# Attention with a KV cache on one core: 16 KB loads, a block transpose on VectorE, P*V in 32-row array tiles, and the projection in token groups

## The chip, the cores and the metric

The kernel runs on one core of one Trainium2 chip. The time is the device time of one execution in microseconds. A kernel's time is the median of its runs; a comparison is a ratio with a 95% interval, from runs of both kernels on the same chip.

## The reference

32 sequences, 4 new tokens each (128 tokens in all), 32 query heads on 4 key/value heads, 2048 cached keys of width 128, all in bfloat16:

```python
B, Sq, D = 32, 4, 1024
Hq, Hkv, Sk, Dh = 32, 4, 2048, 128
q = (x @ wq).reshape(B, Sq, Hq, Dh).transpose(0, 2, 1, 3)
k, v = repeat(k_cache, 8, axis=1), repeat(v_cache, 8, axis=1)
scores = einsum("bhqd,bhkd->bhqk", q, k) * Dh ** -0.5
o = einsum("bhqk,bhkd->bhqd", softmax(scores), v)
out = o.transpose(0, 2, 1, 3).reshape(B, Sq, Hq * Dh) @ wo
```

K and V are 67.1 MB each, `wq` and `wo` 8.4 MB each: 151 MB to read for very little arithmetic. "Batch" below means one of the 32 sequences. Its 4 tokens x 32 heads are 128 rows of scores, 32 for each key/value head.

## The kernel before

For each batch: K is transposed on TensorE in eight "fills" of eight 128x128 transposes into a ring of four PSUM banks; VectorE and ScalarE evacuate the fills to `KT_sb`; the score product fills `ps_s`; VectorE takes the maximum and ScalarE the exponential; P is transposed on TensorE by a product with a diagonal that also normalises; P*V uses the whole array, 128 keys per weight load. One projection of all 128 tokens ends the kernel.

```python
# loads: rows of 16 keys x 128 x 2 bytes = 4 KB
def k_src(b): return k_cache[b].rearrange("g (p t) d -> p g (t d)", p=128)
def v_src(b): return v_cache[b].rearrange("g (p t) d -> p g (t d)", p=128)
# SyncE: four K loads a batch, one for each key/value head, two batches ahead
# GpSimd: one V load a batch, after P*V of batch b - 3, and one 256 KB piece of wo
...
def do_tr_fills(b):                     # P transposed and normalised on TensorE
    wait exp(b), diag(b)
    for f in range(4):
        ring_wait(j)
        for q in range(4):
            t = f * 4 + q
            eng.matmul(dst[:, q * 128:(q + 1) * 128],
                       lhsT=P_sb[:, t * 128:(t + 1) * 128], rhs=diag[:, b % 2, :])
...
def do_pv(b):                           # 4 x 16 = 64 pairs of weight load and matmul
    for g in range(G):
        for t in range(NKT):
            eng.matmul(ps_o[:, 32 * g:32 * (g + 1)],
                       lhsT=V_sb[:, vs, g, t * Dh:(t + 1) * Dh],
                       rhs=PT_sb[:, t, 32 * g:32 * (g + 1)],
                       start=(t == 0), stop=(t == NKT - 1))
...
for i in range(B):                      # order of TensorE's program
    qk(i)                               # 4 column tiles of 32, 16 matmuls of 512 columns
    if i >= 1: do_pv(i - 1)
    if i + 2 < B: do_kt_fills(i + 2)
    do_tr_fills(i)
do_pv(B - 1)
for c in range(2):                      # the projection, once, at the end
    for h in range(Hq):
        eng.matmul(ps_s[:, c * 512:(c + 1) * 512], lhsT=oT_sb[:, h, :],
                   rhs=wo_view[:, h, c * 512:(c + 1) * 512], ...)
```

(Waits and marks are cut, and the calls are shortened.)

## Time and profile before

| kernel before | |
|---|---|
| time, median of 2 runs | 410.25 us (409.25 to 411.25) |
| profiled span, granted clock | 409.6 us, 0.925 |
| bytes read | 151.3 MB, 402 to 408 GB/s from slice 5 to slice 36 |
| tail with hardly any load | about 37 us, of it 16.0 us projection |

These lines are from the profile's page. In it PE is TensorE's matmuls, PEld its weight loads, DVE VectorE, ACT ScalarE, POOL GpSimd, SP SyncE. The first four give the span, the busy time of each engine, and two rows of the table of 40 equal slices of 10.2 us (granted TensorE clock in tenths; GB/s of all loads). Then comes the queue that carries the engines' own instructions (packets, MB, share), and the engines' shares of the chain that ended last.

```profile
span 409.6 us, 12650 instructions
PE 306.7 (75%) x5448; PEld 251.4 (61%) x5448; DVE 244.7 (60%) x390; ACT 197.2 (48%) x230; POOL 42.0 (10%) x70
...
PEclk9799799998999899999999999997998989889679
...
GB/s 307 400 387 401 408 408 407 407 406 407 407 407 408 405 406 407 406 407 407 408 404 407 407 407 406 407 407 406 407 406 407 407 407 408 403 402 308 38 2 26
...
q8 instruction: 44, 0.72, 0.7%
...
DMA 53%; PE 28%; issue 6%; SPq 5%; DVE 4%; ACT 3%; ACTq 0%; DVEq 0%
```

The flat row of GB/s, 402 to 408 from slice 5 to slice 36, says that the loads bind: no compute engine is above 75%. The end of the row is the tail. Queue 8: 44 packets of 16 KB, each 256 instructions of TensorE (5448 matmuls and as many weight loads are 42.6 such blocks).

Next are groups of instructions: count, then busy us and mean ns of one, then the engine's idle time just before them and what ended most of it.

```profile
L539 ACT ACTIVATE pp_sb<-ps_s,negmx 128x2048 bf16<-128x2048 f32 x32 | 62.9, 1967 | 98.7 <-DVE negmx L484 98.7
L481 DVE TENSOR_REDUCE mx<-ps_s 128x1 f32<-128x2048 f32 x32 | 73.3, 2292 | 43.8 <-PE ps_s L397 43.8
...
L346 PE MATMUL ps_o<-pp_sb,V_sb 128*128 128x32 bf16 x2048 | 57.4, 178 | 11.5 <-DMA V_sb<-in_v_cache_dram 7.0
...
L397 PE MATMUL ps_s<-KT_sb,QT_sb 128*32 128x512 bf16 x512 | 34.7, 391 | 2.6 <-ACT QT_sb L522 0.8
```

The view of waits sums, for each engine and line, what it waited for (us in all, times, longest):

```profile
PE ps_c L312 <- DMA K_sb<-in_k_cache_dram: 15.1, 13, 1.6
...
PE ps_b L312 <- issue: 7.9, 4, 2.6
PE ps_a L312 <- issue: 7.6, 3, 2.9
```

"Issue" is time in which an engine waits for nothing that the profile shows. Where do those stops come from? In the instruction records of TensorE, 16 gaps of over 0.3 us (27 us in all, median 1.75) lie at one and the same place, the 193rd of every 256 instructions. After 15 of the 16, TensorE goes on 2.3 to 2.6 us after a packet of queue 8 starts. So they belong to the fetch of instructions, not to the data.

The timeline of the end gives start, duration, engine, line and operation:

```profile
388.14 1.87 PE L346 MATMUL ps_o<-pp_sb,V_sb 128*128 128x32 bf16 x64 [0.88 <-ACT pp_sb L446]
...
390.44 15.95 PE L418 MATMUL ps_s<-w_sb,oT_sb 128*128 128x512 bf16 x64 [0.43 <-issue]
```

### The profile page before, as it was taken

To read this page: it belongs to the slowest core of one execution; us is meant where nothing else is said; L and a number is where in the kernel's file an instruction comes from. 1 tells how busy PE (TensorE), PEld (TensorE's weight loads), DVE (VectorE), ACT (ScalarE), POOL (GpSimd) and SP (SyncE) were. 2 spreads that over 40 slices of the span, in tenths; PEclk is the share of its full clock that TensorE was granted. 3 is DMA by queue.
4 is the path that set the end of the run, shared out by engine and by line. 5 is a ranking of instruction groups with operands and counts; after the bars stand their busy time and mean duration, and the time that the engine had idled before them with its cause. 6 is when DMAs were issued, how large, how long until landed. Compare 5 with 4: busy or idle time off the path is not lost.

```text
span 409.6 us, 12650 instructions
## 1 busy us (share of the span) xinstructions
PE 306.7 (75%) x5448; PEld 251.4 (61%) x5448; DVE 244.7 (60%) x390; ACT 197.2 (48%) x230; POOL 42.0 (10%) x70
## 2 busy tenths in 40 slices
PE   4576877988777687577777777759876787775596
PEld 4476766867655576466666566548765676674442
DVE  2113286786666587677766776745875867765400
ACT  1213066474555555555555455553555555545300
POOL 0001011110100111111111111110110111120000
PEclk9799799998999899999999999997998989889679
DMA  8999999999999999999999999999999999997000
GB/s 307 400 387 401 408 408 407 407 406 407 407 407 408 405 406 407 406 407 407 408 404 407 407 407 406 407 407 406 407 406 407 407 407 408 403 402 308 38 2 26
DMA packets 42390, 152.33 MB, mean 372 GB/s; under 512 B 3168, under 2 KB 3168, under 8 KB 42336
## 3 DMA queue, kind: packets, MB, share of 16 engines
q0 software_dynamic: 19456, 75.50, 46.3%
q1 hardware_dynamic: 21728, 71.84, 44.7%
q10 hardware_dynamic: 1152, 4.19, 2.6%
q8 instruction: 44, 0.72, 0.7%
q14 instruction: 10, 0.08, 0.1%
HBM read 151.26 MB, written 0.26 MB: 370 GB/s over the span
## 4 chain that ended last, share of the span: by engine, by line
DMA 53%; PE 28%; issue 6%; SPq 5%; DVE 4%; ACT 3%; ACTq 0%; DVEq 0%
DMA K_sb<-in_k_cache_dram 32%; DMA V_sb<-in_v_cache_dram 15%; DMA w_sb<-in_wq_dram 6%; PE ps_o L346 5%; PE ps_s L418 4%; PE ps_o L312 4%; PE ps_s L397 3%; SPq L278 3%; PE ps_c L312 3%; PE ps_a L312 3%; PE ps_b L312 2%; SPq L283 2%; ACT KT_sb L446 2%; DVE mx L481 2%; PE ps_s L371 2%
## 5 line engine op out<-in xcount | busy, mean ns | idle before, releaser
L539 ACT ACTIVATE pp_sb<-ps_s,negmx 128x2048 bf16<-128x2048 f32 x32 | 62.9, 1967 | 98.7 <-DVE negmx L484 98.7
L481 DVE TENSOR_REDUCE mx<-ps_s 128x1 f32<-128x2048 f32 x32 | 73.3, 2292 | 43.8 <-PE ps_s L397 43.8
L346 PEld LDWEIGHTS ps_o<-pp_sb,V_sb 128*128 128x128 bf16 x2048 | 53.9, 96 | 25.9 <-issue 16.6
L346 PE MATMUL ps_o<-pp_sb,V_sb 128*128 128x32 bf16 x2048 | 57.4, 178 | 11.5 <-DMA V_sb<-in_v_cache_dram 7.0
L312 PE MATMUL ps_c<-ident,K_sb 128*128 128x128 bf16 x512 | 43.6, 232 | 19.7 <-DMA K_sb<-in_k_cache_dram 15.1
L268 POOL DMA_DIRECT2D V_sb<-in_v_cache_dram x32 | 23.8, 745 | 303.1 <-PE ps_o L346 274.4
L312 PE MATMUL ps_a<-ident,K_sb 128*128 128x128 bf16 x512 | 43.3, 232 | 13.7 <-issue 7.6
L444 DVE COPY KT_sb<-ps_b 128x1024 bf16<-128x1024 bf16 x64 | 43.7, 684 | 12.0 <-PE ps_b L312 11.9
L446 ACT ACTIVATE KT_sb<-ps_a 128x1024 bf16<-128x1024 bf16 x32 | 32.6, 1019 | 37.1 <-PE ps_a L312 37.0
L312 PE MATMUL ps_b<-ident,K_sb 128*128 128x128 bf16 x512 | 43.9, 233 | 7.9 <-issue 7.9
L312 PEld LDWEIGHTS ps_c<-ident,K_sb 128*128 128x128 bf16 x512 | 34.1, 105 | 21.6 <-DMA K_sb<-in_k_cache_dram 19.5
L312 PE MATMUL ps_o<-ident,K_sb 128*128 128x128 bf16 x512 | 43.1, 232 | 3.2 <-DVE KT_sb L444 3.1
L312 PEld LDWEIGHTS ps_a<-ident,K_sb 128*128 128x128 bf16 x512 | 32.9, 104 | 17.6 <-issue 12.0
L446 ACT ACTIVATE KT_sb<-ps_c 128x1024 bf16<-128x1024 bf16 x32 | 32.7, 1022 | 20.9 <-PE ps_c L312 20.9
L312 PEld LDWEIGHTS ps_b<-ident,K_sb 128*128 128x128 bf16 x512 | 34.7, 105 | 9.1 <-issue 8.5
L312 PEld LDWEIGHTS ps_o<-ident,K_sb 128*128 128x128 bf16 x512 | 34.2, 105 | 6.9 <-DVE KT_sb L444 4.4
L444 DVE CAST pp_sb<-ps_a 128x512 bf16<-128x512 f32 x32 | 22.1, 691 | 27.2 <-PE ps_a L328 27.2
L397 PE MATMUL ps_s<-KT_sb,QT_sb 128*32 128x512 bf16 x512 | 34.7, 391 | 2.6 <-ACT QT_sb L522 0.8
L446 ACT ACTIVATE KT_sb<-ps_o 128x1024 bf16<-128x1024 bf16 x32 | 32.7, 1023 | 0.0
L444 DVE COPY KT_sb<-ps_a 128x1024 bf16<-128x1024 bf16 x32 | 21.9, 685 | 10.2 <-PE ps_a L312 10.2
L371 PE MATMUL ps_s<-pp_sb,w_sb 128*128 128x128 bf16 x256 | 19.8, 255 | 10.0 <-DMA w_sb<-in_wq_dram 10.0
L371 PEld LDWEIGHTS ps_s<-pp_sb,w_sb 128*128 128x128 bf16 x256 | 19.2, 118 | 10.6 <-DMA w_sb<-in_wq_dram 10.6
(36 smaller groups left out, 288.9 us busy)
## 6 DMA issues: line engine op xcount, KB each, us to landing
V_sb<-in_v_cache_dram POOLq DMA_DIRECT2D x32, 2048.0 KB, 26.4
K_sb<-in_k_cache_dram SPq DMA_DIRECT2D x120, 512.0 KB, 14.6
w_sb<-in_wq_dram SPq DMA_DIRECT2D x4, 2048.0 KB, 25.2
w_sb<-in_wo_dram POOLq DMA_DIRECT2D x32, 256.0 KB, 26.1
K_sb<-in_k_cache_dram ACTq DMA_DIRECT2D x8, 512.0 KB, 10.7
pp_sb<-in_x_dram SPq DMA_DIRECT2D x1, 256.0 KB, 4.2
out_dram<-pp_sb SPq DMA_DIRECT2D x1, 256.0 KB, 2.0
```

The costliest lines, as they stand in the source:

```text
L268: eng.dma_start(V_sb[:, vs, :, :], v_src(b)).then_inc(s_v[vs], 16)
L278: eng.dma_start(wq_sb[:, :, c * WQC:(c + 1) * WQC], wq_v[:, :, c * WQC:(c + 1) * WQC]).then_inc(s_wq[c], 16)
L283: eng.dma_start(K_sb[:, ks, g, :], k_src(b)[:, g, :]).then_inc(s_k[ks][g], 16)
L312: ins = eng.transpose(dst[:, q * 128:(q + 1) * 128], K_sb[:, ks, g, t * Dh:(t + 1) * Dh], ident[:, :],)
L346: ins = eng.matmul(ps_o[:, 32 * g:32 * (g + 1)], lhsT=V_sb[:, vs, g, t * Dh:(t + 1) * Dh], rhs=PT_sb[:, t, 32 * g:32 * (g + 1)], start=(t ...
L371: ins = eng.matmul(ps_s[:, col:col + 128], lhsT=wq_sb[:, kt, h * Dh:(h + 1) * Dh], rhs=xT_sb[:, kt, :], start=(kt == 0), stop=(kt == KT - 1),)
L397: ins = eng.matmul(ps_s[32 * g:32 * (g + 1), c * 512:(c + 1) * 512], lhsT=QT_sb[:, i, REP * g:REP * (g + 1), :], rhs=KT_sb[:, kts, g, c * ...
L418: ins = eng.matmul(ps_s[:, c * 512:(c + 1) * 512], lhsT=oT_sb[:, h, :], rhs=wo_view[:, h, c * 512:(c + 1) * 512], start=(h == 0), stop=(h ...
L444: ins = eng.tensor_copy(dst, src)
L446: ins = eng.activation(dst, src, ACT.Copy)
L481: ins = eng.tensor_reduce(mx[:, i:i + 1], ps_s[:, :], AX.X, ALU.max)
L539: ins = eng.activation(P_sb, ps_s[:, :], ACT.Exp, bias=negmx[:, i:i + 1], scale=scale, accum_out=ssum[:, i:i + 1],)
```

## The change

The whole kernel is written anew. The intent: larger rows for the loads, no transposing of P on TensorE, no long projection at the end.

- K and V are loaded with 64 neighbouring keys of one head in each partition: rows of 16 KB. Partition 32g + r holds keys 64r to 64r + 63 of head g.
- So the keys of a head lie on 32 partitions only. P is normalised and transposed in 32x32 blocks on VectorE, and P*V contracts 32 keys at a time on a 32-row tile of the array: 64 steps x 4 heads = 256 pairs instead of 64.
- P*V writes the first 32 columns of the four ring banks, so it waits for the last K evacuations, and the next fills wait for O's evacuation (now on ScalarE, ahead of the exponential).
- `wq` is loaded first and alone, in 16 KB rows; all loads are in one queue. `wo` is loaded early.
- The projection runs for 32 tokens at a time after batches 7, 15, 23 and 31, in four column tiles.

```diff
-            return v_cache[b].rearrange("g (p t) d -> p g (t d)", p=128)
+                V_sb[:, b % NVB, :, :], v_cache[b].rearrange("g (r t) d -> (g r) t d", r=R)),
 ...
-                        ins = eng.matmul(dst[:, q * 128:(q + 1) * 128],
-                            lhsT=P_sb[:, t * 128:(t + 1) * 128], rhs=diag[:, b % 2, :])
+            p.op("dve", lambda e: e.tensor_scalar(P_sb[:, :], P_sb[:, :], rinv[:, i:i + 1], None, op0=ALU.mult), ...)
+            p.op("dve", lambda e: e.transpose(PT_sb[:, i % 2, :, :].rearrange("p t q -> p (t q)"), P_sb[:, :]), ...)
 ...
-                    for t in range(NKT):                      # 16 for each of 4 heads
-                        ins = eng.matmul(ps_o[:, 32 * g:32 * (g + 1)],
-                            lhsT=V_sb[:, vs, g, t * Dh:(t + 1) * Dh],
-                            rhs=PT_sb[:, t, 32 * g:32 * (g + 1)], ...)
+            for t in range(T):                                # 64 for each of 4 heads
+                for g in range(G):
+                    p.op("pe", lambda e, t=t, g=g: e.matmul(ps_r[:, g, 0:32],
+                        lhsT=V_sb[32 * g:32 * (g + 1), i % NVB, t, :],
+                        rhs=PT_sb[32 * g:32 * (g + 1), i % 2, t, :], ...), ...)
 ...
+            for h in range(Hq):                               # oproj(n): tokens 32n to 32n + 31
+                for j in range(4):
+                    p.op("pe", lambda e, h=h, j=j: e.matmul(ps_r[32 * j:32 * (j + 1), 0, 0:NC],
+                        lhsT=oT_sb[:, h, 32 * n:32 * (n + 1)],
+                        rhs=wo_sb[:, h, NC * j:NC * (j + 1)], tile_position=(0, 32 * j), ...), ...)
 ...
+        for i in range(B):                                    # order of the programs
+            pe_qk(i); softmax_max(i)
+            if i >= 1: pe_pv(i - 1); ot(i - 1)
+            if i + AHEAD < B: pe_fills(i + AHEAD)
+            if i >= 1 and i % OG == 0: oproj(i // OG - 1)
+            softmax_exp(i); ev(i + AHEAD, dve_fs); ev(i + AHEAD, act_fs)
+            softmax_pt(i)
```

(Cut and shortened; the remainder is the same algorithm in another frame.)

## The prediction

> **What bounds the kernel now.** DMA. In the 40 slices it moves a flat 405 to 408 GB/s from the start to slice 36: 151.3 MB, 372 of 409.6 us. The rest is a tail after the last V lands (timeline: two softmax rounds, the last P*V, a projection of 16.0 us). No compute engine is at its limit (PE 75%, DVE 60%, ACT 48%); one batch costs 10.3 us of DMA.
>
> **What the change takes away.**
> - DMA: packet records show 86 ns for 2 KB, 162 ns for 4 KB, so about 10 ns fixed. For 16 KB I estimate 618 ns, 424 GB/s: 357 us in all.
> - Start: wq comes first and alone, so batch 0 starts about 12 us sooner. Tail: only the last token group's projection, 4 to 5 us instead of 16.
> - 16 P-transposing matmuls and four evacuations per batch.
>
> Were DMA still the bound: about 375 us. I don't think it will be.
>
> **What it adds, per batch.**
> - P*V becomes 256 weight-load/matmul pairs instead of 64. On the whole array pairs start 25.2 ns apart (P*V's records). [...]this trace's score matmuls agree (3.3 ns between column tiles). So P*V takes about 2 us if row tiles overlap, 6.5 us if not.
> - VectorE: normalising P [...]and the block transpose. [...]I estimate [...]like the max reduction: 2.3 us.
> - A serial loop. P*V writes the ring banks, so it waits for K's last evacuations; ScalarE does O's evacuation, exp, then five evacuations, in order. From the end of one P*V to the start of the next: 0.45 + 2.2 + 5 x 0.92 = 7.3 us on ScalarE; via evacuation 5, normalisation and transpose about 8.5 us on VectorE. Period = P*V + 8.5 us: 10.5 us at best.
> - Instructions: PE goes from about 350 to 690 per batch. PE's program comes in 16 KB blocks (256 instructions; queue 8, 44 packets). In the records PE stops at the same place of every 256 when a fetch is late, and resumes 2.4 to 2.6 us after its packet starts; under full DMA load fetches are never less than 6.4 us apart. Now that is hidden under DMA ("issue", 0.9 to 3 us a stop). After, a P*V of 512 instructions outruns the fetched blocks once or twice per batch, estimate 2 to 5 us each batch.
>
> So the period is 12.5 to 15.5 us (middle 14), above the 9.9 us of DMA: 32 x 14 + 33 us start + 10 us tail = about 490 us.
>
> **Predicted: 490 us, range 385 to 565. Faster by over 2%: 0.25; within 2%: 0.05; slower by over 2%: 0.70.**
>
> **What would show it.** DMA near 300 GB/s in the middle; 16 KB packets of about 620 ns (if still 4 KB, no gain of rate). Queue 8 near 90 packets. The chain of waits made of VectorE transpose, ScalarE evacuations, P*V and "issue" in P*V. P*V's matmuls in bursts 6 ns apart with stops of 2 to 5 us. Start and tail together some 20 us shorter: right even if the total is wrong.
>
> **What would make it wrong.** If fetches are quicker with fewer data queues or further ahead, and row tiles overlap fully, the period is about 10.5 us, the time 375 to 390 us. If row tiles don't overlap, or a 32-row weight load is slow, or the clock halves in the waits, it passes 540 us.

The forecast's sum came to 490 us: 32 periods of 14 us, 33 us of start, 10 us of tail. The 14 us are P*V's 2, the loop's 8.5 and, in the middle, 3.5 for late fetches. The trace before shows this: score matmuls in neighbouring column tiles start 4 ns apart in the median (294 of 384 steps 1 to 5 ns, the others 14 to 18; the 3.3 ns are near the first four of a batch, 3.1 in the mean). With two starts of 4 ns for each pair of weight load and matmul, 256 pairs would take 2.0 us (an estimate; that row tiles overlap in the same way was the assumption). The maximum over 2048 columns takes 2.29 us, from which the transpose is estimated. The 2.2 us are the exponential and the read of its sum (1.97 and 0.19 us); evacuations on ScalarE start some 0.92 us apart. The 0.45 us for O's evacuation are the estimate (VectorE took 0.28 us for it before).

## More of the kernel before

On one core a single run has no known state (fast or slow). The runs told here as "one look" are such single runs, each beside one run of the kernel before, and are used only where the difference is far larger than a few per cent.

## The result

| | before | after |
|---|---|---|
| median time | 410.25 us (2 runs) | 609.08 us (2 runs, 606.88 to 611.28) |
| ratio | 1 | 1.4848 (1.4695 to 1.5001) |
| profiled span, clock | 409.6 us, 0.925 | 605.1 us, 0.718 |
| stops at the 193rd of 256 instructions | 16, 27 us | 45, 176 us |

A ratio is the mean time of one kernel's fast runs over the mean of the other's of the same rounds, so it is not quite the ratio of the medians quoted beside it.

The page after, with the same lines as before and the queue that carries the loads added:

```profile
span 605.1 us, 23784 instructions
PE 329.0 (54%) x11528; PEld 291.8 (48%) x11528; DVE 246.4 (41%) x265; ACT 229.7 (38%) x261; POOL 7.1 (1%) x18
...
PEclk9997675777767677776667876757777766777756
...
GB/s 367 427 430 418 238 386 393 364 338 246 235 154 279 214 264 222 239 226 222 244 263 277 283 135 178 273 260 278 263 234 226 236 168 279 249 218 234 142 3 8
...
q1 hardware_dynamic: 14192, 151.29, 63.4%
q8 instruction: 90, 1.47, 0.9%
...
PE 41%; issue 29%; DVE 20%; DMA 6%; ACT 3%; SPq 0%
```

No engine and no queue is at its limit any more (PE 54%, the queue of the loads 63.4%). The loads reach 427 to 430 GB/s while the buffers fill in the first slices, more than before, and from the tenth slice on fall to between 135 and 283, because the buffers come free too late (SyncE waits 503 us in all for the fills before it can issue the next K). The chain of waits has lost the loads (53% to 6%) and gained "issue" (6% to 29%). The instruction queue carries 90 packets instead of 44 (11528 matmuls and as many weight loads are 90.1 blocks of 256).

The groups after:

```profile
L207 PE MATMUL ps_r<-ident,K_sb 128*128 128x128 bf16 x2048 | 184.4, 276 | 35.7 <-ACT oT_sb L254 14.3
L246 PE MATMUL ps_r<-PT_sb,V_sb 32*128 32x32 bf16 x8192 | 78.1, 182 | 221.1 <-issue 150.8
...
L273 DVE STREAM_TRANSPOSE PT_sb<-P_sb 128x2048 bf16<-128x2048 bf16 x32 | 74.0, 2311 | 1.1
...
L271 DVE TENSOR_SCALAR P_sb<-P_sb,rinv 128x2048 bf16<-128x2048 bf16 x32 | 24.1, 754 | 1.1
```

The waits after:

```profile
PE ps_r L246 <- issue: 150.8, 37, 5.5
PE ps_r L246 <- DVE PT_sb L273: 70.3, 32, 5.7
...
PE ps_r L207 <- issue: 14.0, 7, 3.9
```

P*V waits 150.8 us for "issue" in 37 stops, about one a batch: its own instructions are late. The timeline shows it. Two batches follow each other here, and below them the last batch:

```profile
303.54 1.23 PE L246 MATMUL ps_r<-PT_sb,V_sb 32*128 32x32 bf16 x133 [1.93 <-DVE PT_sb L273]
...
308.74 1.18 PE L246 MATMUL ps_r<-PT_sb,V_sb 32*128 32x32 bf16 x123 [3.97 <-issue]
...
309.99 0.28 ACT L254 ACTIVATE oT_sb<-ps_r 128x128 bf16<-128x128 f32 x1 [7.84 <-PE ps_r L246]
310.17 1.96 ACT L265 ACTIVATE P_sb<-ps_s,negmx 128x2048 bf16<-128x2048 f32 x1
...
310.42 0.69 PE L207 MATMUL ps_r<-ident,K_sb 128*128 128x128 bf16 x5 [0.49 <-ACT oT_sb L254]
...
314.83 6.05 PE L207 MATMUL ps_r<-ident,K_sb 128*128 128x128 bf16 x59 [3.73 <-issue]
...
321.22 2.31 DVE L273 STREAM_TRANSPOSE PT_sb<-P_sb 128x2048 bf16<-128x2048 bf16 x1
...
323.59 1.62 PE L246 MATMUL ps_r<-PT_sb,V_sb 32*128 32x32 bf16 x180 [1.73 <-DVE PT_sb L273]
...
330.03 0.79 PE L246 MATMUL ps_r<-PT_sb,V_sb 32*128 32x32 bf16 x76 [4.82 <-issue]
...
591.35 1.67 PE L246 MATMUL ps_r<-PT_sb,V_sb 32*128 32x32 bf16 x181 [5.69 <-DVE PT_sb L273]
...
595.40 0.79 PE L246 MATMUL ps_r<-PT_sb,V_sb 32*128 32x32 bf16 x75 [2.38 <-issue]
...
596.59 5.41 PE L284 MATMUL ps_r<-w_sb,oT_sb 128*32 128x256 bf16 x128 [0.40 <-ACT oT_sb L254]
```

P*V does 133 pairs in about 1.2 us, stands still for 4 us, and does the other 123. While it stands, ScalarE and the fills wait behind it (the 7.84 us before O's evacuation), so the stop is paid in full. The stop moves by 47 pairs from one batch to the next (133, then 180): from one P*V to the next TensorE has 674 instructions in the records (932 or 930 where a projection lies between). That is 94 short of three blocks of 256, so a stop that stays at the same place of each 256 moves by 94 instructions, or 47 pairs. In the last batch no loads run, and the stop is 2.4 us.

The start times in the records give one batch, as a mean over batches 0 to 27: period 18.0 us, of which P*V takes 7.3 us from its first to its last start (5.3 us of stops, 2.0 us of matmuls), and 10.7 us pass from there to the next P*V.

### The profile page after: what moved, and what is told of

It reads as the page before. It is cut to its first block, busy times and chain, and to the rows that moved or that the text cites. A ratio compares the mean times of both kernels' runs of the same rounds, so it can differ in the third digit from the quotient of the medians.

```text
span 605.1 us, 23784 instructions
## 1 busy us (share of the span) xinstructions
PE 329.0 (54%) x11528; PEld 291.8 (48%) x11528; DVE 246.4 (41%) x265; ACT 229.7 (38%) x261; POOL 7.1 (1%) x18
## 3 DMA queue, kind: packets, MB, share of 16 engines
q1 hardware_dynamic: 14192, 151.29, 63.4%
## 4 chain that ended last, share of the span: by engine, by line
PE 41%; issue 29%; DVE 20%; DMA 6%; ACT 3%; SPq 0%
PE ps_r L207 25%; PE ps_r L246 13%; DVE PT_sb L273 12%; DMA K_sb<-in_k_cache_dram 6%; DVE P_sb L271 4%; DVE KT_sb L219 3%; PE ps_r L284 3%; ACT oT_sb L254 2%; ACT P_sb L265 1%; ACT KT_sb L221 1%; DVE rinv L270 0%; SPq L127 0%; DVE o_sb L292 0%; SPq L124 0%
## 5 line engine op out<-in xcount | busy, mean ns | idle before, releaser
L207 PE MATMUL ps_r<-ident,K_sb 128*128 128x128 bf16 x2048 | 184.4, 276 | 35.7 <-ACT oT_sb L254 14.3
L246 PE MATMUL ps_r<-PT_sb,V_sb 32*128 32x32 bf16 x8192 | 78.1, 182 | 221.1 <-issue 150.8
L207 PEld LDWEIGHTS ps_r<-ident,K_sb 128*128 128x128 bf16 x2048 | 178.0, 129 | 40.5 <-issue 32.2
L246 PEld LDWEIGHTS ps_r<-PT_sb,V_sb 32*128 32x128 bf16 x8192 | 71.3, 94 | 240.4 <-issue 154.3
L219 DVE COPY KT_sb<-ps_r 128x1024 bf16<-128x1024 bf16 x96 | 66.4, 691 | 290.0 <-PE ps_r L207 290.0
L221 ACT ACTIVATE KT_sb<-ps_r 128x1024 bf16<-128x1024 bf16 x160 | 155.0, 1025 | 44.6 <-PE ps_r L207 42.1
L273 DVE STREAM_TRANSPOSE PT_sb<-P_sb 128x2048 bf16<-128x2048 bf16 x32 | 74.0, 2311 | 1.1
L265 ACT ACTIVATE P_sb<-ps_s,negmx 128x2048 bf16<-128x2048 f32 x32 | 62.8, 1961 | 1.5 <-DVE negmx L261 1.5
L271 DVE TENSOR_SCALAR P_sb<-P_sb,rinv 128x2048 bf16<-128x2048 bf16 x32 | 24.1, 754 | 1.1
L284 PE MATMUL ps_r<-w_sb,oT_sb 128*32 128x256 bf16 x512 | 16.6, 292 | 3.5 <-issue 2.6
```

The costliest lines, as they stand in the source:

```text
L207: p.op("pe", lambda e, b=b, f=f, q=q, t=t: e.transpose(ring[f % 4][:, q * 128:(q + 1) * 128], K_sb[:, b % NKB, t, :], ident[:, :]), waits ...
L219: p.op("dve", lambda e: e.tensor_copy(dst, src), waits, ("kt", b, f))
L221: p.op("act", lambda e: e.activation(dst, src, ACT.Copy), waits, ("kt", b, f))
L246: p.op("pe", lambda e, t=t, g=g: e.matmul(ps_r[:, g, 0:32], lhsT=V_sb[32 * g:32 * (g + 1), i % NVB, t, :], rhs=PT_sb[32 * g:32 * (g + 1), ...
L265: p.op("act", lambda e: e.activation(P_sb[:, :], ps_s[:, :], ACT.Exp, bias=negmx[:, i:i + 1], scale=scale, accum_out=ssum[:, i:i + 1]), [( ...
L271: p.op("dve", lambda e: e.tensor_scalar(P_sb[:, :], P_sb[:, :], rinv[:, i:i + 1], None, op0=ALU.mult), [("rinv", i)], ("pn", i))
```

## The experiments

The theory (A): TensorE's instructions arrive too slowly. A batch has twice as many, a fetch of 256 comes too late, and each late fetch stops P*V for about 5 us. The rivals: (B) the chain of steps through VectorE and ScalarE makes the period by itself, with P*V's matmuls a small part; (A2) a stop is as long without loads as with them; (A3) it is long because the fetch stands behind 16 KB data packets. The first four runs are one look each, on one chip, beside one run of the kernel before of 408.97 us.

### A quarter of P*V (e1_quarter_pv)

Wrong (relative error 0.83): only 64 of the 256 pairs of each batch, all else as after.

```diff
-            for t in range(T):
+            for t in range(T // 4):
```

> The changed kernel with P*V cut to a quarter (64 of 256 pairs per batch; a wrong result on purpose; loads, transposes, softmax, evacuations unchanged). Theory A, instruction supply: PE now runs about 306 instructions per batch, P*V fits in what is already fetched, its stops of 5 us vanish; with the stops gone the clock stays higher and K's transposes shorten; the period falls under 10 us and the loads bind: 370 to 410 us. Theory B, the serial loop between P*V, ScalarE and VectorE: only P*V's own 2.0 us shrink to 0.5: 605 - 32 x 1.5 = about 555 us.

Measured: 406.02 us (span 404.2, clock 0.873). No stop in P*V is left, and queue 8 has 42 packets. Theory A's interval holds, B's does not. A transposing matmul of K takes 242 ns in the mean instead of 276. TensorE's largest waits are now for the transposed P and for evacuations; in six places the fills wait for K:

```profile
PE ps_r L246 <- DVE PT_sb L273: 71.6, 32, 7.1
...
PE ps_r L207 <- DMA K_sb<-in_k_cache_dram: 25.8, 6, 6.5
```

The timeline of one batch of this run:

```profile
304.24 2.25 DVE L260 TENSOR_REDUCE mx<-ps_s 128x1 f32<-128x2048 f32 x1
304.37 0.56 PEld L246 LDWEIGHTS ps_r<-PT_sb,V_sb 32*128 32x128 bf16 x64 [2.59 <-DVE PT_sb L273]
...
306.72 1.97 ACT L265 ACTIVATE P_sb<-ps_s,negmx 128x2048 bf16<-128x2048 f32 x1 [1.32 <-DVE negmx L261]
...
308.68 4.67 ACT L221 ACTIVATE KT_sb<-ps_r 128x1024 bf16<-128x1024 bf16 x5
...
310.40 0.69 DVE L219 COPY KT_sb<-ps_r 128x1024 bf16<-128x1024 bf16 x1 [2.52 <-PE ps_r L207]
...
311.99 2.31 DVE L273 STREAM_TRANSPOSE PT_sb<-P_sb 128x2048 bf16<-128x2048 bf16 x1
...
314.35 0.56 PEld L246 LDWEIGHTS ps_r<-PT_sb,V_sb 32*128 32x128 bf16 x64 [2.59 <-DVE PT_sb L273]
```

This is the serial loop without stops: maximum, exponential, ScalarE's first evacuation, the fill behind it, VectorE's last evacuation, normalisation, transpose, and the next maximum waits for that transpose. It takes 9.98 us, and P*V runs beside the maximum. The loads of a batch need about 9.9 us (an estimate: 4.19 MB at the 424 GB/s of the prediction). So A's guess that the loads would bind holds only in part: the loop sets the pace of most batches, the loads that of a few early ones (18.7 us of the waits for K fall while `wo` lands, up to 121 us), and the three projections add some 5 to 8 us each. Without stops this design came to 406 us: the faster loads are given back. (The quarter takes 0.5 us where the whole P*V takes 2.0. That the whole one would still fit beside the 2.25 us maximum is argued, not run.)

### Half of P*V twice (e2_more_pairs)

Correct: the first half of P*V is done, then the whole of it over again; 384 pairs a batch.

```diff
-            for t in range(T):
+            for n, t in enumerate(list(range(T // 2)) + list(range(T))):
```

> The changed kernel with the first half of P*V done twice (384 pairs per batch, result stays right). Theory A: 256 more instructions are one more fetched block per batch, about 5.2 us: 605 + 32 x 5.2 = about 770 us (740 to 800), and some 122 packets on queue 8. Theory B: 128 pairs more at 8 ns are 1.0 us per batch: about 640 us.

Measured: 739.4 us (clock 0.678), a hair under A's interval; B's is far off. Queue 8 has 122 packets; 73 stops at the 193rd instruction take 282 us. The same wait as above:

```profile
PE ps_r L246 <- issue: 262.8, 69, 6.1
```

The 256 more instructions of a batch cost (739.4 - 609.1) / 32 = 4.1 us, and the array needs 1.0 us for them (128 pairs at 8 ns). Three points lie close to one line: 290 instructions from one P*V to the next gave 406 us, 674 gave 609, 930 gave 739 (16.5 and 15.9 ns for each added instruction).

### No loads after the first buffers (e3_no_loads)

Wrong (relative error 1.10): K is loaded for batches 0 and 1 and V for 0 to 2 only; later batches use what lies in the buffers.

```diff
+            if b >= NKB:
+                p.at[("k", b)] = p.at[("k", b % NKB)]
+                return
 ... (the same for V)
```

> The changed kernel with K and V loaded for the first two and three batches only (wrong result on purpose; instructions of PE unchanged). If a late block waits behind the loads' packets (theory A1), the stop in P*V falls from 5.0 us to about 2.5 us, as in the last three batches of the changed kernel: 605 - 32 x 2.7 = about 515 us (490 to 530). If a block takes as long whatever the load (A2): 590 to 605 us.

Measured: 506.94 us (clock 0.757), in A's interval, outside A2's. There are as many fetches (90 packets), but 38 stops take 88 us, median 2.36 instead of 4.65. The period is 14.5 us.

```profile
PE ps_r L252 <- issue: 77.3, 35, 5.3
```

The loads thus cost half of the stop. From the start of a fetch's packet to TensorE going on, it is 2.4 us in this run as in the run after (median 2.44 and 2.36); the added time lies before the packet starts. Even with almost no loads this kernel is 98 us slower than the kernel before.

### Rows of 4 KB (e4_4kb_rows)

Correct: each K and V load in four parts, with rows of 4 KB instead of 16 KB.

```diff
-            p.dma("sp", lambda e: e.dma_start(K_sb[:, b % NKB, :, :], ...))
+            for c in range(4):
+                p.dma("sp", lambda e, c=c: e.dma_start(K_sb[:, b % NKB, 16 * c:16 * c + 16, :], ...))
 ... (the same for V)
```

> The changed kernel with each load of K and V in four pieces of 4 KB rows, as before had (result stays right). If it is the 16 KB packets that make the blocks late (A3): the stops in P*V shorten by 1 us or more, 565 us or less. If packet size doesn't matter to them: 600 to 615 us; the packet records then show only the loads' own rate fall from 16384 B per 611 ns to 4096 B per about 162 ns.

Measured: 616.34 us, just above the interval without an effect; 47 stops, 185 us, median 4.66. The size of the data packets does not make the stop long, and A3 falls. The rows do matter for the rate while the loads run freely: 400 and 413 GB/s in the second and third slice against 427 and 430.

```profile
PE ps_r L250 <- issue: 159.4, 38, 5.7
```

### Do the other parts of the change pay by themselves?

The kernel before was given parts of the change without the 32-row P*V. These runs have 3 rounds (b5_spread 5); all are correct.

**Projection in token groups (b1_groups).**

```diff
+                if i >= 1 and i % OG == 0:
+                    do_oproj(i // OG - 1, i)      # 32 tokens, four column tiles, after tr_fills(i)
-            (the projection of 128 tokens at the end)
+            do_oproj(NOG - 1, B - 1)
-                    issue_wo(1)
+                    issue_wo(8)                    # wo whole by batch 5
```

> One part alone on the kernel before: the projection in four token groups (wo loaded at batches 2 to 5, the last group's product alone at the end). The loads stay the bound; the tail loses the difference between a projection of 16.0 us and one of 5.4 us (the last group in the changed kernel): 410 - 10 to 12 = about 398 us (394 to 402). PE's instructions per batch hardly change. If the middle groups' projections disturb the loads, 402 us or more.

Measured: 413.9 us, ratio 1.0058 (1.002 to 1.0096); a miss. The last projection did shrink, to 5.19 us. But P*V of batch 31 ended at 402.7 us instead of 390. The second group's projection (its matmuls start from 243.5 to 249.8 us, with a stop of 2.6 us for instructions among them) runs into a slice at 274 GB/s. What the tail gained was lost before it.

**The same, in pieces (b5_spread).** From batch 8 on each batch projects four heads of the finished group, and VectorE adds the pieces in a float buffer.

```diff
+                if i >= OG:
+                    do_oproj(i // OG - 1, i, 4 * (i % OG), 4 * (i % OG) + 4, f"chunk{i}")
                 do_tr_fills(i)
```

> The kernel before with the projection in token groups again, but in pieces: from batch 8 on each batch projects four heads of the group of eight batches that is complete (16 matmuls of 32x256 instead of 128 at once), VectorE adds the piece to a float sum, and only the last group is projected whole at the end. If the groups of b1 failed because 128 matmuls at once hold TensorE for 5 us and the loads behind it, the loads now flow at 404 to 408 GB/s to the end, P*V of batch 31 ends near 390 to 392 us, the last projection takes about 5 us instead of 16, and the time is 398 to 402 us (ratio 0.97 to 0.98). If any further work between exp and the next score product delays the loads (a piece costs about 1 us of that path in each batch), P*V of batch 31 ends at 395 us or later and the time is 405 to 415 us.

Measured: 411.4 us against 408.88, ratio 1.0061 (1.0037 to 1.0086); a miss again. The time and the end of P*V (401.0 us) lie in the rival's intervals, but its reason, loads that flow late, explains little of them, as the bytes below show. The last score product but one starts at 380.21 us (370.66 before), and from there to the last P*V it takes 19.0 us (17.5 before). That is 11 us later in all, against 12.3 us less projection (3.7 us at the end), so next to nothing is left:

```profile
380.21 1.05 PE L430 MATMUL ps_s<-KT_sb,QT_sb 128*32 128x512 bf16 x16
...
399.23 1.75 PE L361 MATMUL ps_o<-pp_sb,V_sb 128*128 128x32 bf16 x64 [0.89 <-ACT pp_sb L469]
...
401.56 3.68 PE L376 MATMUL ps_s<-w_sb,oT_sb 128*32 128x256 bf16 x128 [0.58 <-DVE oT_sb L476]
```

Summing the packet records, the loads are only 0.8 MB (2 us) behind the kernel before at 370 us. So most of the 9.5 us is not bytes. The waits point to their order: a group needs `wo` whole by batch 8, and between 107 and 138 us, while `wo` lands (up to 132 us), P*V waits 20.5 us for V in three stops.

```profile
PE ps_o L361 <- DMA V_sb<-in_v_cache_dram: 20.9, 4, 10.3
```

In the kernel before these waits are 7.0 us in all, the first of them at 328 us. At the end the last K lands at 376.9 us here and at 363.8 before, where 1.3 MB of `wo` came after it. That the order alone costs the 9.5 us was not run.

**16 KB rows for K and wq as well (b2_k16).** On top of b1; the exponential writes P's columns in the order that V's rows have, 8 bytes apart.

```diff
-                    P_sb,
+                    P_sb.rearrange("p (t r a) -> p t a r", r=R, a=4),
```

> The kernel before with the changed kernel's cheap parts: token groups, wq first and by 16 KB rows, K by 16 KB rows; P is still transposed on TensorE with the diagonal, V stays in 4 KB rows and P*V in 64 whole-array pairs (exp writes P's columns in V's order, so no instruction is added). PE stays near 350 instructions per batch, so theory A expects no new stops. Loads: 75.5 MB at 16384 B per 611 ns x 16 (429 GB/s), 75.8 MB at about 405: 363 us, plus 2 us start and a tail of 12 to 18 us: 375 to 388 us.

Measured: 474.18 us, ratio 1.1536 (1.1504 to 1.1567); a miss. The exponential took 4.82 us instead of 1.97:

```profile
L540 ACT ACTIVATE pp_sb<-ps_s,negmx 128x2048 bf16<-128x2048 f32 x32 | 154.1, 4817 | 127.6 <-DVE negmx L491 127.6
```

**All loads in one queue (b3_one_queue).**

```diff
-                eng.dma_start(V_sb[:, vs, :, :], v_src(b)).then_inc(s_v[vs], 16)    # GpSimd
+                load_v(b - KT_AHEAD)                                                # SyncE, after K(b)
```

> The kernel before with one part of the changed kernel: V issued from SyncE in one queue with K, in the order K(b+2), V(b), instead of from GpSimd. Bytes, packet size and PE's instructions stay. In before, V of batch 28 lands only at 361.7 us because K runs ahead in its own queue, so three P*V and two softmax rounds follow the last load (372 us). If the order of landing sets that tail, it shortens by about 10 us: 398 to 402 us. If the tail is the chain of the last two batches whatever lands first: 408 to 412 us.

Measured: 409.55 us, ratio 0.9991 (0.9947 to 1.0036): the same. The order of landing is not what sets the tail of the kernel before; its last two softmax rounds and the projection are.

**One queue, 16 KB rows for K and wq (b4_k16_queue).** Instead of the exponential, the score product takes K's columns 64 bytes apart.

```diff
-                            rhs=KT_sb[:, kts, g, c * 512:(c + 1) * 512],
+                            rhs=KT_sb[:, kts, g, 4 * c:4 * c + 4, :, :].rearrange("p t a r -> p t r a"),
```

> b3 with wq first and K and wq by 16 KB rows; the score product reads K's transpose in V's key order (steps of 64 bytes in the moving operand), so exp and the evacuations stay as they were. Loads: 8 us less than b3 (K and wq 429 GB/s instead of 405). If the stepped read costs nothing, b3 minus 8: about 392 us (385 to 396). If it slows the score product (1.05 us for 16 matmuls) by a factor of 2 to 4, up to 3 us more per batch, PE and the loop no longer hide it: 400 to 460 us.

Measured: 433.39 us, ratio 1.0577 (1.0535 to 1.0619), in the interval for a slowed score product. A score matmul took 1057 ns instead of 391:

```profile
L393 PE MATMUL ps_s<-KT_sb,QT_sb 128*32 128x512 bf16 x512 | 118.7, 1057 | 1.6
```

In both kernels the larger rows of K bring another order of the keys, and putting the order right costs more than the rows give. The change escapes this by giving V the same order, and that is what leads to 32 keys per weight load and 256 pairs. No version was found that beats the kernel before.

## Why the prediction was right and wrong

The direction and the bottleneck were right, the size was not: 490 us with 565 as the upper end, measured 609.

What held:

- "DMA" as the bound before, and a bound that moves away from DMA after: 53% of the chain before, 6% after.
- 16 KB packets: 611 ns measured, 618 estimated. 90 packets in queue 8, as predicted.
- Row tiles overlap: 256 pairs in 2.0 us, predicted "about 2 us". The trace has 8 ns from one matmul to the next, each with a weight load of its own; on the whole array pairs started 25.2 ns apart.
- The transpose, 2.31 us (predicted 2.3, from the maximum's 2.29 us for as many columns). The normalisation took 0.75 us.
- The start: batch 0's score product at 38.2 us instead of 47.7 (9.5 us sooner, predicted 12), and the last projection 5.4 us instead of 16.0 (predicted 4 to 5); together 20 us, as predicted.

What failed is the sum "32 x 14": the period was 18.0 us (and the loads in the middle ran at 135 to 283 GB/s, not "near 300"). Two of its terms were too small.

1. "outruns the fetched blocks once or twice per batch, estimate 2 to 5 us each batch". The number of late fetches was right (1.2 stops in a P*V). The size was not: P*V lost 5.3 us, and the fills another 0.5, against 3.5 in the middle of the estimate. The estimate took the stops of the trace before (0.9 to 3 us each), where fetches had 8.5 us between them in the median; in 12 of the 16 stops the packet had started before TensorE ran dry, after the change in 8 of 45. After the change a P*V uses up 512 instructions in 2 us, and much more of a fetch shows: about 4.7 us under load and 2.4 without (e3). This term is (5.8 - 3.5) x 32 = 74 us.
2. "about 8.5 us on VectorE" from the end of one P*V to the next. The mean was 10.7. In the records, where no projection lies between, it is the time of the 64 transposes, from first to last start, plus 3.3 to 4.1 us. Three batches whose fills took 4.6 to 4.8 us (granted clock 0.73 to 0.76) have 8.6 to 8.8 us, so the sum of the steps was about right; 17 of 28 batches have 9.4 to 10.1 us, with fills of 5.4 to 6.3 us, in which up to 53 of the 63 steps take 107 ns instead of 56. Stops in the fills of seven batches (five of them over 1 us) and three projections make up the rest. The prediction had named the cause, "or the clock halves in the waits", only as a way to be wrong: the granted clock was 0.718. The trace's clock records are 1.0 or 0.5 and nothing else, 0.5 for 341 of 594 us (in the kernel before 62 of 399). K's transposes start 107 ns apart at 0.5 and 56 ns at 1.0, in the median. Of the 31 stops of over 4 us, 24 begin at 1.0 and all end at 0.5; of the 14 shorter ones only 2 go from 1.0 to 0.5. One stretch at 0.5 begins at 306.6 us, within the stop from 304.6 to 308.7 us shown above. In this trace the half clock follows the long stops. This term is 2.2 x 32 = 70 us, of which 0.5 x 32 is the fills' share that is counted above already.

The two make 128 us if every batch is taken at the mean. From the first score product to the end of the last P*V the trace has 558 us, which is 110 over the 32 x 14 predicted, because the first round and the last three batches (no loads, no fills: 10 to 14 us) are shorter. The start was 5 us later than the 33 us predicted, the tail as predicted.

The range's lower end rested on "If fetches are quicker with fewer data queues or further ahead". After the change, with one data queue, the stops grew. One queue by itself did not do that: in the one profiled execution of b3 the stops are 11, 14 us in all, against 16 and 27 us. But the "375 to 390 us" given for that case was too low as well. With the stops gone (e1) the serial loop of 10 us, the projections and the early waits for K give 406.

Open: what holds a fetch back by the added 2.3 us under load before its packet starts. A block's packet starts after TensorE passes the place of a possible stop one block earlier: in the median 1.1 us after it in e3, 2.8 us in the run after and 2.9 us in e4, so it is not the size of the data packets. What it is, no run shows.

## What to carry to other kernels

Before splitting a product into smaller tiles, count the engine's instructions per microsecond: here 512 of them ran in 2 us, but a late fetch of 256 stopped TensorE for 4.7 us in the median, so four times the pairs at about the same array time (2.0 us against 1.7) cost 5 us a batch. Look in the trace for stops at one place modulo the size of a fetch; if they are already there and hidden, more instructions can bring them to the surface, and longer, as they did here (16 stops of 1.75 us in the median became 45 of 4.65). And a part of a change that seems free (larger rows, an earlier projection) should be tried by itself: here none of five versions gained, because another step or, as far as the traces tell, the order of the loads took the gain back.
